# A transformer block with modulation: the first scale load waits on SP until x tile 1 has landed

## The chip, the cores and the metric

The kernel runs on one core of one Trainium2 chip. The metric is the device time of one execution in microseconds (us); three executions of the kernel before took 243.2, 244.03 and 244.05 us, median 244.03. One further execution was recorded by the hardware profiler; all rows of profiles are from such executions.

The engines are named as in the profile: PE (matrix multiply; PEld is its weight load, which overlaps the multiply), DVE (vector), ACT (scalar), POOL (GpSimd) and SP (which here only issues loads and stores). Each has its own list of instructions, which it works through in order, and waits for the others at semaphores.

## The reference

B = 2 sequences of N = 256 tokens, D = 1152, two heads of 576, a hidden width of 4608, all in bf16:

```python
mod = (_silu(c) @ w_mod).reshape(B, 6, 1, D)
shift_a, scale_a, gate_a, shift_m, scale_m, gate_m = [mod[:, i] for i in range(6)]
h = _layernorm(x, axis=-1) * (1 + scale_a) + shift_a
qkv = (h @ wqkv).reshape(B, N, 3, H, Dh)
attn = _softmax(jnp.einsum('bqhd,bkhd->bhqk', q, k) * Dh ** (-0.5), axis=-1)
a = jnp.einsum('bhqk,bkhd->bqhd', attn, v).reshape(B, N, D) @ wo
x = x + gate_a * a
h2 = _layernorm(x, axis=-1) * (1 + scale_m) + shift_m
m = _gelu(h2 @ w_fc1) @ w_fc2
return x + gate_m * m
```

## The kernel before

The 512 tokens are four x tiles of 128 tokens (two for each sequence), each 128 partitions x 1152 columns, 288 KB. The width 1152 is nine chunks of 128. Weights come from device memory into five rotating buffers ("wide"), each holding one 1152 x 1152 matrix.

All instructions of an engine keep the order in which the Python code makes them; a loop at the end of the kernel ties each to the one before it on its engine. So the order of SP's loads is the order of the calls. At the start SP issues:

- the four x tiles, in the order 0, 1, 3, 2 (L85, L86), into `x_sb`;
- then, alternating, the modulation weights that make the attention scale, `w_scale_a`, in five groups of columns (`SGROUPS`: chunks 0-1, 2-3, 4-5, 6-7 and 8; L107), and the rows of the key weights `w_k` that belong to the same chunks (L104, first for the columns of six key panels, the remaining three panels last);
- then the shift and query weights (L129, L134), and through `load_rows` (L120) gate, value and output weights, and later those of the second half of the block.

ACT issues the small load of `c` (L84) and nothing else in this stage. POOL loads nothing in this stage.

The front of the kernel turns x into its normalized, scaled and transposed form and starts the key product at once. `act_stats` (L206) computes the sums of tiles 0 and 2 on ACT, two passes over a tile each; `stats_piece` (L193, L195) those of tiles 1 and 3 on DVE, in three pieces and a closing instruction. From these come the reciprocal deviations: `act_mean_eps` (L213 on DVE, L342 and L218 on POOL), `act_root` (L335) and `root_exp` (L338) on ACT, `pool_rsqrt` (L329) on POOL for tile 3. `norm1` (L233, DVE) writes the normalized tile, PE transposes it by chunks (L264), and `modulate` (L270 on DVE, L272 on ACT) multiplies by the scale into `hT0`.

The scale itself is a product on PE: `scale_group` (L247) multiplies a group of `w_scale_a` columns with silu(c), nine matmuls of two columns for each chunk. So the first group of scale columns is wanted just before the first `modulate`, and `k_step` (L280) then multiplies a chunk of `hT0` with the rows of `w_k` for six key panels. The order in which PE alternates between these is written out by hand (L345 to L404). Before there is work PE runs multiplications of zeros (L173).

After that: the remaining key panels (L309), shift (L416), query (L521), scores, softmax, values (L599), attention output (L640, L693), the second layernorm, and the two large products of the MLP (L746 and L802).

Of the kernel before, what the change touches and what calls it, by code (L numbers as in the profile page):

```python
# [19 lines left out]
def kernel(  # L20
# [11 lines left out]
    nc = tc.nc  # L32
    B, N, D = x.shape
# [3 lines left out]
    P = 128  # L37
    T = B * N
    NT = T // P
    TPB = N // P  # L40
# [9 lines left out]
    WAIT_FOR = mybir.DependencyInfo(mybir.DependencyClass.Sync, mybir.DependencyReason.DATA)  # L50
# [16 lines left out]
    x_v = x.rearrange("b (p l) d -> p b l d", l=TPB)  # L67
    out_v = out.rearrange("b (p l) d -> p b l d", l=TPB)
    c_v = c.rearrange("b (k p) -> (b k) p", p=P)
    wqkv_v = wqkv.rearrange("(k p) n -> p k n", p=P)  # L70
# [7 lines left out]
    def wide_tile(name):  # L78
        return wide.tile([P, KD, D], BF16, name=name, tag="wide")


    x_sb = act.tile([P, NT, D], BF16, name="x_sb", tag="x_sb")
    c_sb = act.tile([B * KD, P], BF16, name="c_sb")
    nc.scalar.dma_start(c_sb[:], c_v)  # L84
    for t in (0, 1, 3, 2):  # L85
        nc.sync.dma_start(x_sb[:, t, :], x_v[:, t // TPB, t % TPB, :])  # L86

    zeros = const.tile([P, T], BF16, name="zeros")
    nc.vector.memset(zeros[:], 0.0)
# [9 lines left out]
    KM1 = 6  # L99
    w_scale_a = wide_tile("w_scale_a")  # L100
    w_k = wide_tile("w_k")

    def load_k(k0, k1, c0, c1):
        nc.sync.dma_start(w_k[:, k0:k1, c0:c1], wqkv_v[:, k0:k1, D + c0:D + c1])  # L104

    for k0, k1 in SGROUPS:
        nc.sync.dma_start(  # L107
            w_scale_a[:, :, k0 * P:k1 * P],
            wmod_v[:, :, S_SCALE_A * D + k0 * P:S_SCALE_A * D + k1 * P],
        )  # L110
        for a, z in [(0, 1), (1, 2)] if k0 == 0 else [(k0, k1)]:
            load_k(a, z, 0, KM1 * P)
    load_k(0, KD, KM1 * P, D)

    first_load = {}

# [279 lines left out]
    for k in range(3, KD):  # L396
        split = 2 if k == 5 else 0
        k_step(k, 0, T, 0, split)
        if k in (3, 5, 7):
            k1 = min(k + 3, KD)  # L400
# [456 lines left out]
```

## Time and profile before

| What | Value |
|---|---|
| Runs, median (lowest to highest) | 244.03 us (243.2 to 244.05) |
| The profiled execution's own time | 243.19 us |
| Its span, first to last instruction | 241.4 us |
| PE busy | 236.4 us (98%) |
| DVE, ACT, POOL busy | 91.4, 59.9, 28.3 us |
| Loads on SP's queue | 50.14 MB, 62.5% of 16 DMA engines' span |
| Granted PE clock | 1.0 |

The span leaves out 1.8 us of the execution that lie before and after it. In the rows of the profile, a group names its line in the code, engine, operation, and the tile it writes and those it reads ("pm<-sT,w_scale_a"), with a count. "SPq" is the issue of a load by SP: its length is the time SP spends on issuing, not that of the transfer. The profile tells separately how long after the start of an issue the data had landed. "Idle before" is the time for which an engine had nothing to do, with what ended it. The chain of waits is followed back from the last instruction; "issue" in it is time in which the engine waited for nothing that the profile shows. Times in rows count from the start of the span, and the first number of a row is the start, the second the length, both in us.

### The profile page before, as it was taken

Reading aid. Unit: us, or ns where it says so; the run is one execution under the profiler, and the core shown is the slowest. Engines: PE = TensorE matmul, PEld = TensorE weight load, DVE = VectorE, ACT = ScalarE, POOL = GpSimd, SP = SyncE. Lnnn points to the kernel's source line nnn. Section 1 sums busy time; section 2 is a strip of 40 time slices with the busy share of each in tenths; the row PEclk is TensorE's granted clock in tenths of the full one; section 3 lists DMA queues with packets and bytes.
Section 4 is the critical chain, followed back from the end, with each engine's and each line's share of the span. In section 5 each row is a group of like instructions: output and inputs, shape, how many; then the busy total and the mean of one; then the engine's idle time right before and its main releaser. Section 6 shows DMA issues by size and latency. Waiting matters only on the chain.

```text
span 241.4 us, 3978 instructions
## 1 busy us (share of the span) xinstructions
PE 236.4 (98%) x1688; PEld 145.1 (60%) x1698; DVE 91.4 (38%) x193; ACT 59.9 (25%) x121; POOL 28.3 (12%) x47
## 2 busy tenths in 40 slices
PE   8999999999999999999999999999999999999994
PEld 5775444466667665888844444444665566666574
DVE  4842442319325678930003999950010000000001
ACT  6723322307215032770423333222000000000000
POOL 2300000001300324100000000001121111111111
PEclk9999999999999999999999999999999999999999
DMA  6999999997499993739999999999300000000000
GB/s 196 325 317 311 377 366 391 391 391 244 122 331 394 389 274 76 195 65 378 391 391 391 337 326 270 287 327 270 98 16 16 20 16 16 19 18 20 26 21 16
DMA packets 48781, 53.29 MB, mean 221 GB/s; under 512 B 9587, under 2 KB 36475, under 8 KB 48763
## 3 DMA queue, kind: packets, MB, share of 16 engines
q1 hardware_dynamic: 41312, 50.14, 62.5%
q10 hardware_dynamic: 6939, 1.71, 4.6%
q0 software_dynamic: 512, 1.19, 1.8%
q8 instruction: 13, 0.21, 0.4%
q14 instruction: 5, 0.04, 0.1%
HBM read 50.14 MB, written 1.19 MB: 213 GB/s over the span
## 4 chain that ended last, share of the span: by engine, by line
PE 94%; issue 2%; ACT 2%; POOL 1%; DVE 0%; POOLq 0%; DVEq 0%; ACTq 0%
PE pacc L802 29%; PE pacc L746 29%; PE pacc L693 7%; PE pacc L599 7%; PE pq L521 7%; PE pk L280 5%; PE pk L309 2%; PE pa L640 2%; PE ps_s L556 2%; PE pn L416 2%; ACT sink L206 1%; PE pt L264 1%; PE pm L247 1%; PE pg L498 0%; ACT rstd L335 0%
## 5 line engine op out<-in xcount | busy, mean ns | idle before, releaser
L746 PE MATMUL pacc<-hT,w_f 128*128 128x256 bf16 (+1 forms) x427 | 70.3, 325 | 0.3
L802 PE MATMUL pacc<-w_f,gT 128*128 128x384 bf16 (+2 forms) x468 | 70.5, 314 | 0.0
L802 PEld LDWEIGHTS <-gT 128*128 128x128 bf16 x468 | 44.4, 98 | 26.3
L746 PEld LDWEIGHTS <-w_f 128*128 128x128 bf16 x432 | 42.2, 98 | 27.6
L808 DVE TENSOR_TENSOR tmp<-pacc,gate 128x384 f32<-128x384 f32 (+2 forms) x13 | 6.8, 526 | 65.6 <-PE pacc L802 57.0
L778 ACT ACTIVATE gT<-pacc 128x512 bf16<-128x512 f32 x24 | 14.3, 597 | 32.7 <-PE pacc L746 32.7
L469 DVE SCALAR_TENSOR_TENSOR part<-w_gate_m,s,part 128x1152 f32<-128x1152 bf16 x16 | 21.4, 1412 | 0.0
L810 POOL TENSOR_TENSOR o_sb<-tmp,x 128x384 bf16<-128x384 f32 (+1 forms) x12 | 11.7, 972 | 53.9 <-DVE tmp L808 53.9
L693 PE MATMUL pacc<-w_o,big 128*128 128x384 bf16 x108 | 17.9, 326 | 0.0
L521 PE MATMUL pq<-hT,w_q 128*128 128x512 bf16 x79 | 17.7, 379 | 0.1
L599 PE MATMUL pacc<-w_v,hT 128*128 128x384 bf16 x108 | 17.7, 326 | 0.0
L599 PEld LDWEIGHTS <-hT 128*128 128x128 bf16 x108 | 10.5, 98 | 7.1 <-issue 0.2
L693 PEld LDWEIGHTS <-big 128*128 128x128 bf16 x108 | 10.4, 98 | 7.2 <-issue 0.4
L521 PEld LDWEIGHTS <-w_q 128*128 128x128 bf16 x81 | 7.8, 98 | 9.4
L280 PE MATMUL pk<-big,w_k 128*128 128x256 bf16 (+1 forms) x70 | 13.1, 324 | 0.1
L699 POOL TENSOR_TENSOR x<-tmp,x_sb 128x384 f32<-128x384 f32 x8 | 7.3, 912 | 27.0 <-DMA w_scale_m<-in_w_mod_dram 15.0
L467 DVE TENSOR_SCALAR part<-w_gate_m,s 128x1152 f32<-128x1152 bf16 x2 | 1.6, 818 | 21.9 <-DMA w_gate_m<-in_w_mod_dram 21.9
L491 POOL DMA_DIRECT2D gates_dram<-nat_v x2 | 1.1, 534 | 67.7 <-DVE nat_v L489 67.7
L280 PEld LDWEIGHTS <-w_k 128*128 128x128 bf16 x72 | 6.7, 97 | 3.7 <-issue 0.3
L767 ACT ACTIVATE gT<-pacc 128x512 bf16<-128x512 f32 x12 | 6.5, 598 | 9.1 <-PE pacc L746 9.1
L173 PE MATMUL pwarm<-zeros 128*128 128x256 f32 x18 | 7.4, 587 | 1.2 <-DVE eps_t L93 1.2
L512 POOL DMA_DIRECT2D gates_dram<-nat x4 | 2.4, 604 | 49.6 <-DVE nat L509 48.5
(102 smaller groups left out, 165.0 us busy)
## 6 DMA issues: line engine op xcount, KB each, us to landing
w_f<-in_w_fc_dram SPq DMA_DIRECT2D x12, 864.0 KB, 14.1
w_f<-in_w_fc_dram SPq DMA_DIRECT2D x3, 1728.0 KB, 7.9
w_f<-in_w_fc_dram SPq DMA_DIRECT2D x2, 2592.0 KB, 17.4
w_gate_a<-in_w_mod_dram SPq DMA_DIRECT2D x3, 864.0 KB, 12.1
w_v<-in_wqkv_dram SPq DMA_DIRECT2D x3, 864.0 KB, 13.8
w_o<-in_wo_dram SPq DMA_DIRECT2D x3, 864.0 KB, 14.0
w_shift_m<-in_w_mod_dram SPq DMA_DIRECT2D x3, 864.0 KB, 8.6
w_scale_m<-in_w_mod_dram SPq DMA_DIRECT2D x3, 864.0 KB, 13.3
```

Of the source, the lines that this page charges most:

```text
L173: nc.tensor.matmul(dst[:, 0:T // 2], zeros32[:, 0:P], zeros32, start=True, stop=True)
L280: nc.tensor.matmul(pk[m][:, c0:c1], w_k[:, k, m * P:(m + 1) * P], hT0[:, k, c0:c1], start=(k == 0 and c0 == 0), stop=(k == KD - 1), skip_g ...
L469: nc.vector.scalar_tensor_tensor(part[:, b, :], wg[:, k, :], s32[:, k, b:b + 1], part[:, b, :], op0=ALU.mult, op1=ALU.add,)
L521: nc.tensor.matmul(pq[m][:], w_q[:, k, m * P:(m + 1) * P], hT[:, k, :], start=(k == 0), stop=(k == KD - 1), skip_group_check=True,)
L599: nc.tensor.matmul(pacc[:], hT[:, k, t * P:(t + 1) * P], w_v[:, k, pnl * PW:(pnl + 1) * PW], start=(k == 0), stop=(k == KD - 1),)
L693: nc.tensor.matmul(pacc[:], aT[:, k, t * P:(t + 1) * P], w_o[:, k, c0:c1], start=(k == 0), stop=(k == KD - 1),)
L699: (nc.gpsimd if pool_add else nc.vector).tensor_tensor(x1[:, t, c0:c1], tmp[:], x_sb[:, t, c0:c1], op=ALU.add)
L746: nc.tensor.matmul(dst, w_f1[m // KD][:, k, ml * P:(ml + 1) * P], hT[:, k, c0:c1], start=start, stop=(k == KD - 1), **kw,)
L778: nc.scalar.activation(gT[:, m, :], pacc[:], ACT.Gelu_apprx_tanh)
L802: nc.tensor.matmul(pacc[:], gT[:, kk, t * P:(t + 1) * P], w_f2[j][:, r, c0 - n * PW:c0 - n * PW + cw], start=(kk == 0), stop=(kk == KF - 1),)
L808: nc.vector.tensor_tensor(tmp[:], pacc[:], gate_m[:, b, c0:c0 + cw], op=ALU.mult)
L810: (nc.vector if last else nc.gpsimd).tensor_tensor(o_sb[:], tmp[:], x1[:, t, c0:c0 + cw], op=ALU.add)
```

## The change

The four x loads keep their order and place, and their handles are kept in a dictionary. The scale and key loads of the loop over `SGROUPS` are kept in a list. One dependency is added: the first of that list, the load of scale columns for chunks 0 and 1, waits for the landing of x tile 1, the second x load that was issued. SP works in order, so every load behind it on SP comes after that wait as well. No data, size or order of a load changes.

```diff
-    for t in (0, 1, 3, 2):
-        nc.sync.dma_start(x_sb[:, t, :], x_v[:, t // TPB, t % TPB, :])
+    x_load = {t: nc.sync.dma_start(x_sb[:, t, :], x_v[:, t // TPB, t % TPB, :]).ins for t in (0, 1, 3, 2)}
...
     def load_k(k0, k1, c0, c1):
-        nc.sync.dma_start(w_k[:, k0:k1, c0:c1], wqkv_v[:, k0:k1, D + c0:D + c1])
-
+        return nc.sync.dma_start(w_k[:, k0:k1, c0:c1], wqkv_v[:, k0:k1, D + c0:D + c1]).ins
+
+    k_loads = []
     for k0, k1 in SGROUPS:
-        nc.sync.dma_start(
+        k_loads.append(nc.sync.dma_start(
             w_scale_a[:, :, k0 * P:k1 * P],
             wmod_v[:, :, S_SCALE_A * D + k0 * P:S_SCALE_A * D + k1 * P],
-        )
+        ).ins)
         for a, z in [(0, 1), (1, 2)] if k0 == 0 else [(k0, k1)]:
-            load_k(a, z, 0, KM1 * P)
+            k_loads.append(load_k(a, z, 0, KM1 * P))
     load_k(0, KD, KM1 * P, D)
+    tc.add_manual_dep(k_loads[0], x_load[1].name, WAIT_FOR, reason="x first")
```

## The prediction

> **What bounds the kernel now.** I read the page's busy times first, then the chain of waits in order of time, the queue of SP, the DMA traffic in half microseconds, and the timeline of the first 32 us. PE is busy 98% of the span. The chain shows where it isn't yet the bound:
>
> ```profile
> 2.46 3.73 issue
> 6.19 0.02 POOLq L218
> ...
> 6.25 0.24 POOL dm L342
> ...
> 7.23 1.25 ACT sink L206 x2
> 8.48 0.02 issue
> 8.50 1.36 ACT sink L206 x2
> ...
> 10.56 0.42 DVE xn L233
> ...
> 11.03 0.29 PE pt L264 x2
> 11.32 0.44 PE pk L280 x4
> ```
>
> Up to 11.03 the end hangs on the layernorm statistics (x tile 0 on ACT, x tile 1 on DVE, then x tile 2 on ACT); from 11.03 on it is PE almost without a break. So a microsecond lost before 11.03, or a PE stall after it, is a microsecond at the end. The change acts here, on SP's own list of issues:
>
> ```profile
> 0.73 1.81 SPq L86 DMA_DIRECT2D x_sb<-in_x_dram  x4
> 2.58 0.43 SPq L107 DMA_DIRECT2D w_scale_a<-in_w_mod_dram  x1
> 3.06 1.67 SPq L104 DMA_DIRECT2D w_k<-in_wqkv_dram  x2
> 4.77 0.60 SPq L107 DMA_DIRECT2D w_scale_a<-in_w_mod_dram  x1
> 5.41 2.25 SPq L104 DMA_DIRECT2D w_k<-in_wqkv_dram  x1
> ```
>
> The four x issues start at 0.73, 1.17, 1.64 and 2.11; asked one by one, they land 2.9, 3.2, 4.6 and 4.9 us later: tile 0 at 3.6, tile 1 at 4.4, tile 3 at 6.2, tile 2 at 7.0. DVE's statistics of tile 1 start at 4.38, which fits. The first scale load is issued at 2.58 and lands 6.4 us later, at 9.0; its first user is PE's load at 9.04:
>
> ```profile
> 4.38 1.48 DVE L193 BATCH_NORM_STATS2 stats<-x_sb 128x6 f32<-128x384 bf16 x3
> ...
> 9.04 0.52 PEld L247 LDWEIGHTS <-w_scale_a 128*128 128x128 bf16 x18
> ...
> 15.19 0.59 PEld L247 LDWEIGHTS <-w_scale_a 128*128 128x128 bf16 x18
> ```
>
> Of the 6.4 us, most is queueing. The DMA traffic (columns: window, its length, busy time of PE, PEld, DVE, ACT, POOL, clock, DMA share, GB/s):
>
> ```profile
> 3.00:3.50 0.50, 0.50 (x3) 0.30 (x3) 0.00 (x0) 0.09 (x1) 0.00 (x0) 1.00 1.03 392
> 3.50:4.00 0.50, 0.50 (x2) 0.41 (x3) 0.34 (x2) 0.46 (x2) 0.00 (x0) 1.00 1.16 281
> 4.00:4.50 0.50, 0.50 (x3) 0.41 (x2) 0.39 (x3) 0.50 (x1) 0.00 (x0) 1.00 1.15 286
> 4.50:5.00 0.50, 0.50 (x3) 0.41 (x2) 0.50 (x2) 0.48 (x2) 0.00 (x0) 1.00 0.82 189
> 5.00:5.50 0.50, 0.50 (x2) 0.41 (x2) 0.50 (x2) 0.48 (x1) 0.00 (x0) 1.00 0.76 256
> ```
>
> With the windows before (81, 218 and 356 GB/s in 1.5 to 3.0) this adds up to 0.5 x 2059 = 1030 KB by 5.5, while the four x tiles are 4 x 288 KB = 1180 KB. In the trace's packet records, where x rows are 2304 bytes, scale rows 512 and key rows 1536, the first 512-byte packet starts at 5.47 and the last x packet ends at 6.60. The weights, issued from 2.58, move no byte before 5.47: the loads of this queue are served in order.
>
> [...] the first x issue starts at 0.73 and the DMA share is 0 until 1.5, with the first x packet at 1.75, so 1.02 us. I use the trace's value.
>
> **The change part by part.** (a) The four x loads are issued as before; gathering their handles in a dictionary and a list adds no instruction. 0.
>
> (b) SP waits after its fourth x issue (2.54) until tile 1 has landed (4.35 to 4.4), so the scale load's issue moves from 2.58 to about 4.40: 1.82 us later. Behind it on SP stand all five scale loads, the seven key loads, the shift and query loads and everything SP loads later; each can go 1.8 us later. Nothing on ACT's or POOL's queue stands behind it. The x tiles 3 and 2 are already issued.
>
> (c) What that does to the data. At 4.40 the queue has moved 0.5 x (81+218+356+392+281) + 0.4 x 286 = 778 KB, so 402 KB of x are left. At the best rate shown (392 GB/s) they last 1.03 us, until 5.43; at the 260 GB/s of the windows behind, until 5.9. The first scale packet comes at 4.40 + 1.02 = 5.42. Before it was 5.47. So the queue does not run dry, or barely: the 1.82 us come out of SP's lead over the data, not out of the data. That lead is the cover. If it were gone, the whole 1.82 us would count.
>
> (d) A cold start is slower than a queue that is fed already. The trace has one with equally many rows (9 rows x 128 partitions): the fc1 load issued at 96.54 onto an idle queue.
>
> ```profile
> 96.54 0.37 SPq L620 DMA_DIRECT2D w_f<-in_w_fc_dram  x1
> ```
>
> It lands 5.0 us later, first traffic in the slot from 97.50. If the time goes by rows, the scale load lands at 4.40 + 5.0 = 9.4, 0.4 late. If it goes by bytes (576 of 864 KB), it lands at 4.40 + 1.05 + 3.95 x 0.67 = 8.1, 0.9 early. By the queue's view in (c) it lands at 9.0. Bounds of its lateness: -0.9 to +0.4; I take +0.1.
>
> (e) What lateness costs. At PE's 9.04 there is no slack on the scale load itself. But what PE and DVE do next ends in waits for ACT: DVE sits idle 0.2 us for ACT's rstd before the tile 2 normalization at 10.56, and PE's loads 0.4 us before 11.03. So 0.2 us of lateness are free there. After that PE never idles; the next tight place is the scale load for columns 4-5, issued at 7.71, landing 7.4 us later (15.1) and used at 15.19: slack 0.1. Columns 6-7 land at 10.96 + 7.2 = 18.2 for 18.98, column 8 at 21.4 for 22.08, the first shift load at 18.39 + 10.2 = 28.6 for 29.31. The first query load lands at 20.14 + 11.4 = 31.5 for 31.79. A lag of 0.4 that lasted to 15.1 would cost 0.3; a lag of 0.1 costs 0 to 0.05.
>
> (f) SP's lead afterwards. From first scale to second scale issue SP needs 4.77 - 2.58 = 2.19 us, for 960 KB (983 thousand bytes); at the 320 GB/s that the queue then moves these take 3.07 us. So SP gains 0.88 us on the data for every such round, and has its old lead back after about two rounds (1.82 / 0.88), near 11 us. Meanwhile the lead doesn't go below the first packet's 1.02 us: the second scale load, issued at 4.77 + 1.82 = 6.6, can move from 7.6; its turn comes after 983 thousand bytes from 5.45, at 8.5. Cost 0.
>
> (g) A possible gain: x flows at 392 GB/s until 3.5, then at 189 to 286, just from one first-packet latency behind the scale issue (2.58 + 1.02 = 3.6). [...] the change takes that off, and tile 1 lands up to 0.2 earlier. DVE's chain leads ACT's by little: ACT's second pass over tile 0 ends at 6.37, and ACT starts its root at 6.51 because POOL's epsilon came at 6.48. So at most 0.14 us. Tiles 3 and 2 would land earlier by 0.5 to 1.5 us for nothing: ACT is busy until 7.22 before tile 2 (7.0), DVE until 6.14 before tile 3 (6.2). Bounds -0.14 to 0; I take 0.
>
> The sum is 0 (a) + 0.1 at most of (b to e) + 0 (f) + 0 (g): +0.1, within -0.14 and +0.4. The profiled execution has span 241.4 and 1.8 around it, 243.19; it becomes 243.3. The runs' median, 244.03, lies 0.84 above that execution; taken over, the forecast is 244.1.
>
> **The rivals.** *The queue runs dry* (slower). If a restarted queue needs longer than the x that is left to drain, the stream slides as a block: the scale load keeps its 6.4 us, lands at 10.8, PE stands at 9.04 and again at 15.19, and the end moves by 1.82 - 0.05 = 1.8 us: 245.8. For it: the cold start at 96.54 reaches only 135 GB/s in its second quarter microsecond. Against it: 402 KB of x at 4.40 and the first weight byte at 5.47. It decides once the first-packet latency passes some 1.5 us (5.9 - 4.4), and costs what lies above; a partial version, with 0.5 to 1 us lost, gives 244.5 to 245.0.
>
> *x arrives earlier* (g): 0.14 less, 243.9. For it: the rate's fall at 3.5. Against: the two issues behind tile 1 can't speed up tile 0, whose ACT passes carry the chain.
>
> *Faster by more than 1.2 us*: this would need a piece of the front to vanish. The chain's x wait before ACT's first pass ends at 3.63 on tile 0, which the change leaves alone; after it, ACT's own four passes of 1.25 us fill the time. Worked out, nothing gives under 243.9 by mechanism.
>
> **How the numbers follow.** A change of 0.5% (1.2 us) is about what a measurement here can tell from none: the runs before span 243.2 to 244.05. Forecast as it stands, 0.62; x earlier, 0.10; the partial slide, 0.10; the full slide, 0.14; faster by over 0.5%, 0.04. The first three are within 0.5%, 0.82. The range reaches from 243.0, the lower run less the 0.14 of (g), to 245.2, the partial slide with its margin; it leaves out the full slide and the large gain, 0.18.
>
> **What would show it.** Right: SP's scale issue at about 4.4, first PE load of the scale weights at 8.9 to 9.3, DMA traffic without an empty window between 5 and 6, PE's second dense stretch still from about 11.0, and the load for columns 4-5 used at 15.1 to 15.4. (g) shows as tile 2 landing near 5.6 and 350 GB/s or more in 3.5 to 5.0. The slide shows as a window near 0 GB/s around 5.5 and PE's loads at 10.8. The forecast is wrong if tile 1 is seen landing later than 4.4, if the restart needs over 1.5 us, or if the lead is not regained before 15 us.

## The result, and the profile after

The changed kernel takes 245.29 us (median of 6 executions, 244.7 to 245.78); the kernel before, in the same comparison, 243.88. The ratio is 1.006, 95% interval 1.004 to 1.0081: 1.4 us slower, where 0.1 was forecast and the range ended at 245.2. The profiled execution took 244.91 us with a span of 243.1, 1.7 more than the span of before.

SP's issues in the profile after (start, length):

```profile
0.73 1.80 SPq L85 DMA_DIRECT2D x_sb<-in_x_dram  x4
4.38 0.38 SPq L107 DMA_DIRECT2D w_scale_a<-in_w_mod_dram  x1
4.81 1.87 SPq L103 DMA_DIRECT2D w_k<-in_wqkv_dram  x2
6.72 0.43 SPq L107 DMA_DIRECT2D w_scale_a<-in_w_mod_dram  x1
7.20 1.81 SPq L103 DMA_DIRECT2D w_k<-in_wqkv_dram  x1
```

The wait does what the diff says: the first scale load leaves at 4.38, 1.80 us later than before, and the scale and key loads behind it 1.3 to 2.1 later. It lands 5.9 us after its issue, at 10.3; before it was 9.0. PE's loads of scale weights, with the idle time ahead of them in brackets:

```profile
10.31 0.52 PEld L248 LDWEIGHTS <-w_scale_a 128*128 128x128 bf16 x18 [1.44 <-DMA w_scale_a<-in_w_mod_dram]
...
13.94 0.52 PEld L248 LDWEIGHTS <-w_scale_a 128*128 128x128 bf16 x18 [0.45 <-DMA w_scale_a<-in_w_mod_dram]
...
16.98 0.52 PEld L248 LDWEIGHTS <-w_scale_a 128*128 128x128 bf16 x18 [0.28 <-DMA w_scale_a<-in_w_mod_dram]
```

Before, these stood at 9.04, 12.30 and 15.19 with no wait on a load. They are now 1.27, 1.64 and 1.79 later. From the third on nothing more is gained or lost: the last large product stands at 169.68 in the chain of waits, in place of 167.96, 1.72 later. So the whole difference of the two profiles arises in the first 17 us. The chain of waits says the same; ACT's statistics have left it, and loads stand there:

```profile
1.16 3.21 DMA x_sb<-in_x_dram
...
4.38 0.38 SPq L107
...
6.72 7.17 DMA w_scale_a<-in_w_mod_dram
...
13.95 0.60 PE pm L248 x18
...
16.98 0.60 PE pm L248 x18
```

The DMA traffic (the last number is GB/s; columns as in the prediction) shows what the landing hides. Before:

```profile
5.50:6.00 0.50, 0.50 (x2) 0.34 (x2) 0.47 (x2) 0.50 (x1) 0.00 (x0) 1.00 0.96 293
6.00:6.50 0.50, 0.50 (x3) 0.39 (x2) 0.42 (x3) 0.36 (x2) 0.25 (x2) 1.00 1.03 321
6.50:7.00 0.50, 0.50 (x3) 0.41 (x2) 0.50 (x2) 0.48 (x2) 0.23 (x1) 1.00 1.08 328
7.00:7.50 0.50, 0.50 (x3) 0.41 (x2) 0.50 (x2) 0.48 (x2) 0.00 (x0) 1.00 1.17 339
```

After:

```profile
5.00:5.50 0.50, 0.50 (x2) 0.41 (x2) 0.50 (x2) 0.47 (x1) 0.00 (x0) 1.00 0.66 254
5.50:6.00 0.50, 0.50 (x2) 0.35 (x2) 0.47 (x2) 0.50 (x1) 0.00 (x0) 1.00 0.66 113
6.00:6.50 0.50, 0.50 (x3) 0.45 (x2) 0.50 (x3) 0.37 (x2) 0.23 (x2) 1.00 0.74 195
6.50:7.00 0.50, 0.50 (x4) 0.44 (x3) 0.50 (x3) 0.47 (x2) 0.25 (x1) 1.00 0.98 270
7.00:7.50 0.50, 0.50 (x4) 0.43 (x3) 0.50 (x2) 0.47 (x3) 0.00 (x0) 1.00 1.08 305
```

No window is empty, and the first 512-byte packet starts at 5.44, as forecast (5.47 before). But behind it the rate takes some 2 us to climb from 113 to 305 GB/s. From 8 to 12 it is 231, 258, 274 and 263 GB/s against 336, 322, 292 and 338.

Summed over 1.5 to 12, x's faster flow gains 125 KB before 5.5. Then 256 KB are lost up to 8.0 and 262 KB more up to 12, some 390 KB net: 1.2 us at 322 GB/s. This is one execution; a second profile of the same kernel, further down, lost less.

A second thing stands in the list of executions. The PE clock that was granted on average over the whole execution was 0.998 or 1.0 in three of the six (244.7 to 244.98 us) and 0.992 in the other three (245.6 to 245.78).

### The profile page after: what moved, and what is told of

It is laid out like the page before. It is cut to its first block, busy times and chain, and to the rows that moved or that the text cites. A ratio compares the mean times of both kernels' runs of the same rounds, so it can differ in the third digit from the quotient of the medians.

```text
span 243.1 us, 3988 instructions
## 1 busy us (share of the span) xinstructions
PE 236.8 (97%) x1698; PEld 144.6 (59%) x1698; DVE 91.3 (38%) x193; ACT 59.9 (25%) x121; POOL 28.4 (12%) x47
## 4 chain that ended last, share of the span: by engine, by line
PE 93%; DMA 4%; SPq 1%; DVE 0%; issue 0%; DVEq 0%
PE pacc L747 29%; PE pacc L803 29%; PE pacc L694 7%; PE pacc L600 7%; PE pq L522 7%; PE pk L281 4%; DMA w_scale_a<-in_w_mod_dram 3%; PE pk L310 2%; PE pa L641 2%; PE ps_s L557 2%; PE pn L417 2%; DMA x_sb<-in_x_dram 1%; PE pm L248 1%; SPq L103 1%; PE pt L265 1%; PE pg L499 0%
## 5 line engine op out<-in xcount | busy, mean ns | idle before, releaser
L174 PE MATMUL pwarm<-zeros 128*128 128x256 f32 x18 | 6.8, 546 | 1.2 <-DVE eps_t L92 1.2
```

Of the source, the lines that this page charges most:

```text
L174: nc.tensor.matmul(dst[:, 0:T // 2], zeros32[:, 0:P], zeros32, start=True, stop=True)
```

## The experiments

Each edit is one to the changed kernel, except for one run of the kernel before; times are ratios to the kernel before, measured on the same chip. "+" times are the ratio applied to that kernel's median. All of them compute the full result.

### How long may SP be held?

The wait of the changed kernel, with another tile:

```diff
-    tc.add_manual_dep(k_loads[0], x_load[1].name, WAIT_FOR, reason="x first")
+    tc.add_manual_dep(k_loads[0], x_load[0].name, WAIT_FOR, reason="x first")
```

> The first scale load waits on x tile 0 (lands at 3.6) in place of tile 1, so SP is held 1.05 us instead of 1.82. Theory L (what SP is held is lost one for one[...]): first scale load 1.0 later than in the kernel before, PE's columns 4-5 about 1.0 later than 15.2, time +0.9 to +1.0 us. Theory R (a restart of the queue costs a fixed amount, whatever the hold): as in the changed kernel, +1.4 to +1.7. Theory Q of the prediction (only an empty queue costs): 0, at 3.6 some 640 KB of x are left.

Measured: 0.9996 (0.9982 to 1.001), no difference. SP resumes at 3.76, 1.2 us late; the scale load lands at 9.2, and PE's third load of scale weights is 0.15 from where it was (15.19):

```profile
9.27 0.52 PEld L248 LDWEIGHTS <-w_scale_a 128*128 128x128 bf16 x18 [0.32 <-DMA w_scale_a<-in_w_mod_dram]
12.39 0.61 PEld L248 LDWEIGHTS <-w_scale_a 128*128 128x128 bf16 x18
15.34 0.52 PEld L248 LDWEIGHTS <-w_scale_a 128*128 128x128 bf16 x18
```

Theory L and theory R both fall here: 1.2 us of holding cost nothing that shows (0.2 us at most), and 0.6 more cost the 1.4.

With `x_load[2]`, the last tile:

> The first scale load waits on x tile 2, the last one (lands at about 6.5 when no weights are behind it), so SP is held about 3.9 us and the queue runs empty for certain. Theory L: +3.7 to +4.0 us. Theory R: the fixed restart cost of 1.4 to 1.7 plus the empty time, about 2.1 us more than in the changed kernel, so +3.6 to +3.8 too: this run alone doesn't part the two. Theory Q: only the empty time, first scale packet at 7.6 in place of 5.5, so +2.0 to +2.2.

Measured: 1.0101 (1.0079 to 1.0123), +2.5 us. SP resumes at 6.82 onto an empty queue; the scale load lands 4.3 us later, at 11.1, sooner after its issue than in the changed kernel (5.9). L and R, at +3.6 and more, fall again; Q's +2.0 to +2.2 lies within the interval.

With `x_load[3]`:

> The first scale load waits on x tile 3 (lands at 5.6 to 5.9 when no weights are behind it), 1.2 to 1.5 us later than for tile 1. Theory H ([...] 5.9 us from issue to landing, against 4.3 us on the empty queue of the run that waits for tile 2): the scale load lands about 4.4 us after its issue, near 10.1 to 10.3, as in the changed kernel, and the time is +1.3 to +1.8. Theory R (a restart costs its fixed amount on top of the hold): scale load near 11.6, +2.6 to +3.0.

Measured: 1.0086 (1.0067 to 1.0105), +2.1 us. The landing is theory H's, 4.6 us after the issue at 5.63, at 10.2. The time in the median lies between H and R, but two of the four executions are at a PE clock of 0.992 and 0.993; the other two took 245.10, 1.5 us more than the kernel before, as H has it. Why the load takes longer behind the draining x tail (5.9 us in the changed kernel) than here, no run shows. The restart of an empty queue can be seen here by itself (columns as above):

```profile
6.00:6.50 0.50, 0.50 (x3) 0.39 (x2) 0.50 (x3) 0.41 (x2) 0.22 (x1) 1.00 0.00 0
6.50:7.00 0.50, 0.50 (x3) 0.46 (x2) 0.50 (x2) 0.45 (x2) 0.27 (x2) 1.00 0.65 41
7.00:7.50 0.50, 0.50 (x4) 0.43 (x3) 0.50 (x2) 0.47 (x3) 0.00 (x0) 1.00 0.56 84
7.50:8.00 0.50, 0.50 (x4) 0.33 (x2) 0.47 (x3) 0.50 (x1) 0.08 (x1) 1.00 0.80 225
8.00:8.50 0.50, 0.28 (x3) 0.03 (x2) 0.42 (x2) 0.50 (x2) 0.42 (x2) 1.00 0.98 295
```

First packet at 6.68, 1.05 us after the issue; then 1.5 us up to full rate. At 330 GB/s the load's 590 thousand bytes take 1.8 us; its packets took from 6.68 to 9.67, 3.0. So in this run the restart cost 1.05 us to the first packet and about 1.2 more behind it.

### Is it the hold, or what is queued meanwhile?

The wait on tile 1, on the second load in the list (`k_loads[1]`, the first key load):

> The wait on x tile 1 sits on the second load (the first key load); the first scale load is issued freely at 2.58. SP is held from 3.06 to 4.4, 1.3 us. Theory L (SP's lag is what counts): +1.2 us, scale columns 2-3, 4-5 and so on each 1.3 later. Theory C (what counts is how much is queued in the rings while SP is held; here 590 thousand bytes of scale weights stand behind x, until about 7.3): 0, within 0.3 us, first scale load at 9.0 as before.

Measured: 1.0 (0.9988 to 1.0012). The wait for tile 2 on the second scale load (`k_loads[3]`, `x_load[2]`):

> The wait sits on the second scale load and is for x tile 2 (about 7.0); first scale load and the first two key loads go freely. SP is held from 4.77 to 7.0, 2.2 us, more than in the changed kernel. Theory L: +2.0 to +2.2 us. Theory C: the queue then holds x and 983 thousand bytes of weights, until about 8.5, and the next packet can come at 8.0: 0 to +0.3 us.

Measured: 0.9991 (0.9979 to 1.0004). SP's issues there:

```profile
2.57 0.43 SPq L107 DMA_DIRECT2D w_scale_a<-in_w_mod_dram  x1
3.05 1.62 SPq L103 DMA_DIRECT2D w_k<-in_wqkv_dram  x2
6.56 0.38 SPq L107 DMA_DIRECT2D w_scale_a<-in_w_mod_dram  x1
6.98 0.98 SPq L103 DMA_DIRECT2D w_k<-in_wqkv_dram  x1
8.01 0.67 SPq L107 DMA_DIRECT2D w_scale_a<-in_w_mod_dram  x1
```

SP stands still from 4.67 to 6.56, no shorter than in the changed kernel (1.89 and 1.85 us), and is within 0.3 us of its place two loads later (8.01, before 7.71). This settles it against theory L: a hold of this length can be free. The difference from the changed kernel is that here 983 thousand bytes of weights had been issued behind x when the hold began.

### Do the short rows make it?

First the key loads ahead of the scale load, without and with the wait:

```diff
     for k0, k1 in SGROUPS:
+        if k0 == 0:
+            k_loads.append(load_k(0, 1, 0, KM1 * P))
+            k_loads.append(load_k(1, 2, 0, KM1 * P))
         k_loads.append(nc.sync.dma_start(
...
-        for a, z in [(0, 1), (1, 2)] if k0 == 0 else [(k0, k1)]:
-            k_loads.append(load_k(a, z, 0, KM1 * P))
+        if k0 > 0:
+            k_loads.append(load_k(k0, k1, 0, KM1 * P))
```

> No wait; the first two key loads (128 rows of 1536 bytes each) stand ahead of the first scale load (1152 rows of 512 bytes). The scale load then lands about 1.1 us later than in the kernel before (393 thousand bytes at 350 GB/s), near 10.1, so PE starts 1.1 us later: +0.9 to +1.1 us. It serves as the base of the next run.

> As the run before, with the wait on x tile 1 on the first key load: SP is held 1.82 us as in the changed kernel, but the first thing it issues is two loads with few long rows. Theory D (the loss comes from starting with many short rows[...]): 0 to +0.4 us over the run without the wait. Theory R (any restart at this point costs about as much): +1.2 to +1.7 over it.

Measured: 1.0022 (1.0009 to 1.0035) without the wait, +0.5 us and less than expected; 1.0141 (1.0126 to 1.0156) with it. The 2.9 us between the medians are more than either theory has: all four executions with the wait are at a PE clock of 0.991 to 0.993. The same loads at full clock (the run with `fill(11)` below) are 1.3 us over the run without the wait. That is R's amount, and theory D falls. The key loads themselves land only 0.3 and 0.2 later than without the wait, but the scale load behind them 1.4 later (11.7, not 10.3).

Then wider groups, so that a scale row has 1024 bytes, with six multiplications of zeros on PE (`fill(6)`) ahead of the first scale product:

```diff
-    SGROUPS = [(0, 2), (2, 4), (4, 6), (6, 8), (8, 9)]
+    SGROUPS = [(0, 4), (4, 8), (8, 9)]
...
-        for a, z in [(0, 1), (1, 2)] if k0 == 0 else [(k0, k1)]:
+        for a, z in [(0, 1), (1, 2), (2, 4)] if k0 == 0 else [(k0, k1)]:
```

> No wait; scale columns come in groups of four, four and one chunks, so that the rows of the first scale load are 1024 bytes in place of 512 (1152 rows as before, 1180 thousand bytes), with six multiplications of zeros ahead of the first scale product. The first scale load lands about 1.8 us later than before, near 10.8: +1.2 to +1.8 us. It is the base of the next run.

> The run before with the wait on x tile 1 on the first scale load. Theory D2 (the loss is that short rows come at some 400 to 560 rows a microsecond [...]: 512 bytes each are then 220 to 290 GB/s, 1024 bytes each would be over 400): 0 to +0.5 us over the run without the wait. Theory R (a restart costs the same whatever the rows): +0.9 to +1.5 us over it.

Measured: 1.0063 (1.004 to 1.0087) and 1.017 (1.0144 to 1.0197), 2.9 us between the medians. Four of the five executions with the wait are at a clock of 0.990 to 0.993, none of those without; the fifth took 246.87, 1.7 us over the median without. That one too is far over D2's 0 to 0.5: longer rows don't help. The first scale load lands 1.9 us later with the wait (12.8, 10.9).

The trace has sixteen increments of a semaphore for each load, the steps by which its landing is counted. Which part of the transfer an increment stands for, it doesn't show. In the run with wide groups and the wait four come at 12.4 to 12.8, all others by 11.3. In the changed kernel's first scale load two come at 10.0 and 10.3, all others by 8.9. Landing waits for the last: PE's load of scale weights starts at 10.31, the last increment is at 10.27. In the kernel before, the whole load had landed at 8.98; so fourteen of the sixteen were on time in the changed kernel, and the lateness of this landing is that of two. Its second profile, next, says the same: fourteen by 8.98, the others at 9.4 and 10.0.

### What does PE's stall cost, and why do executions differ by 0.9 us?

The changed kernel once more:

> The changed kernel once more, beside the others on one chip. If its profile is typical: scale load issued at 4.4 and landing near 10.3, [...] PE waits of 1.4, 0.4 and 0.3 us on scale loads, +1.2 to +1.7 us. If the late landing was one execution's accident, the scale load lands near 9.0 to 9.4 here and the cost sits in the later loads.

Measured: 1.0052 (1.0034 to 1.007), +1.3 us. The scale load lands at 10.0; PE waits 1.03 us for it and 0.34 for the third:

```profile
10.02 0.52 PEld L248 LDWEIGHTS <-w_scale_a 128*128 128x128 bf16 x18 [1.03 <-DMA w_scale_a<-in_w_mod_dram]
...
16.17 0.52 PEld L248 LDWEIGHTS <-w_scale_a 128*128 128x128 bf16 x18 [0.34 <-DMA w_scale_a<-in_w_mod_dram]
```

The traffic dips as in the first profile (230 KB lost from 5.5 to 8.0), but from 8 to 12 only 26 KB are lost. Net of the gain before 5.5 that is 135 KB, 0.4 us. PE's last product is 0.9 us later than before, and the profiled execution is the fastest of the eight. So the slow stretch from 8 to 12 belongs to the first execution; the dip, the two late increments and the wait for the third load are in both. One of eight executions had a clock of 0.993, and it was the slowest (245.71).

PE filled with multiplications of zeros while it waits:

```diff
+    fill(5)
     pm0, pm1 = [scale_group(k, k + 1, acc_tile) for k in range(2)]
```

> The changed kernel with five multiplications of zeros (about 1.1 us) ahead of the first scale product, so that PE is not idle while it waits for the late scale load. Theory T (two costs add: late scale loads, and in some executions a lowered PE clock after an idle PE): no execution under a clock of 0.995, median +0.9 to +1.2 us against the kernel before, highest run within 1 us of the lowest. Without T (the clock is not of the idle PE's making): executions of 0.992 to 0.993 and of 1.0 to 1.5 us more remain as frequent as in the changed kernel (4 of 14).

> The kernel before with the same five multiplications, loads untouched: only PE's start on the first scale product moves, from 9.05 to about 10.1. It prices the first stall by itself. By the prediction's slack of 0.2 us: +0.8 us. If scale loads later on have slack to give back, less; if PE's place at 15.19 is what counts (slack 0.1, load not late here) the stall still reaches it in full, so +0.8 either way. Same as before would mean that the first late scale load is not what costs the changed kernel its time.

Measured for the changed kernel: 1.0039 (1.0027 to 1.0051), +0.95 us, 244.11 to 245.03, all twelve executions at a clock of 0.998 or more. In the profiled one, the fastest, the first scale load landed at 9.1, before the zeros were done, and PE still waited 0.3 us for the third (16.02) and 0.5 for the fourth. For the kernel before: 1.001 (0.9999 to 1.0021), +0.2 us, not the 0.8 expected, though PE starts on the first scale product 0.92 later:

```profile
9.96 0.52 PEld L247 LDWEIGHTS <-w_scale_a 128*128 128x128 bf16 x18
12.92 0.61 PEld L247 LDWEIGHTS <-w_scale_a 128*128 128x128 bf16 x18
15.78 0.61 PEld L247 LDWEIGHTS <-w_scale_a 128*128 128x128 bf16 x18
```

In this profile the 0.92 have become 0.59 at 15.78 (before: 15.19), and the fastest executions differ by as much (243.71 and 243.14). The medians differ by less, so part of that stall is probably there in many executions of the kernel before; in this one the load itself landed only at 9.5. A stall of 0.92 us at the first scale product by itself thus costs 0.2 us in the median. In all three profiles of the changed kernel, with and without the zeros, PE waits again for the third scale load, at 16.0 to 17.0. Most of the 0.95 us is therefore likely to come from the later loads; how late the first one was in executions without a profile is not known.

In the run with the key loads first and the wait, PE's idle time was longest, and its profile shows the clock (third number from the end of a row):

```profile
11.00:12.00 1.00, 0.28 (x11) 0.29 (x12) 0.00 (x0) 0.00 (x0) 0.00 (x0) 1.00 1.12 284
12.00:13.00 1.00, 1.00 (x18) 0.68 (x15) 0.83 (x5) 0.00 (x0) 0.00 (x0) 0.67 0.96 301
13.00:14.00 1.00, 1.00 (x7) 0.69 (x6) 0.33 (x2) 0.00 (x0) 0.00 (x0) 0.50 1.05 295
14.00:15.00 1.00, 1.00 (x8) 0.76 (x7) 0.19 (x1) 0.00 (x0) 0.00 (x0) 0.50 1.14 307
15.00:16.00 1.00, 1.00 (x7) 0.79 (x6) 0.88 (x3) 0.47 (x1) 0.00 (x0) 0.62 1.09 333
```

PE had been idle for 2.84 us up to 11.71. Then it gets half its clock, and does 7 to 8 matmuls a microsecond. A window with mean 0.67 has two thirds of a microsecond at 0.5, one with 0.62 three quarters: in all 3.4 us at half clock. The same with `fill(11)` at that place:

> The run with the key loads first and the wait on the first of them, with eleven multiplications of zeros (2.4 us) where PE stood idle for 2.8 us. Loads are as there. Theory T (idle PE lowers its clock to 0.5 for about 3 us afterwards): no execution under 0.995, and 0.8 to 1.3 us less than without the multiplications, 245.6 to 246.1. Without T: 246.7 to 247.0 as there.

Measured: 1.0075 (1.0063 to 1.0088), 245.26 to 245.47 in all five executions, clock 0.999 or more, against 246.7 to 247.0 at 0.991 to 0.993 without: 1.6 us less with the first loads as late as before (scale load at 11.5). The same windows:

```profile
12.00:13.00 1.00, 0.91 (x14) 0.78 (x13) 0.96 (x5) 0.00 (x0) 0.00 (x0) 1.00 1.11 317
13.00:14.00 1.00, 0.99 (x11) 0.70 (x9) 0.60 (x3) 0.09 (x1) 0.00 (x0) 1.00 1.05 304
```

And the run that waits on tile 3, with `fill(6)`:

> The run that waits on x tile 3, with six multiplications of zeros (1.3 us) ahead of the first scale product. Theory T: no execution under 0.995 (two of four were), median at the level of its undisturbed executions, 245.1 or little less. Theory G for its loads: 2.1 us missing, +1.5 to +2.1 against the kernel before.

Measured: 1.0073 (1.0059 to 1.0087), +1.8 us, no clock under 0.998 (two of four without the fill). What theory T says of the clock came true in all three; the saving of 1.6 us is more than its 0.8 to 1.3. The half clock came here after 2.84 us of idle time. It came after 1.40 (1.49 for the weight load), with 1.22 two microseconds earlier, in the profile of the run with the wait on tile 3 in the next section:

```profile
10.44 0.52 PEld L251 LDWEIGHTS <-w_scale_a 128*128 128x128 bf16 x18 [1.49 <-DMA w_scale_a<-in_w_mod_dram]
...
12.00:13.00 1.00, 1.00 (x7) 0.78 (x6) 0.06 (x1) 0.00 (x0) 0.00 (x0) 0.50 1.05 370
```

The length of one idle time doesn't decide it, though. The run that waits for the last tile stood idle for 2.2 us in its profile, and none of its four executions had a low clock. The wide groups with the wait had six zeros, but PE stood idle for another 2.6 us behind them in the profile, which shows no low clock; the four other executions had one. The kernel before had a low clock, 0.993, in 3 of the 102 executions measured beside these runs.

### How much must be queued?

From the runs so far theory G was formed: 1.05 us to the first packet and 1.1 behind it must be covered by what is still queued when SP resumes; what is missing is lost. Two more runs, with the key loads first and going freely and the first scale load waiting (`k_loads[2]`), for tile 1 and for tile 3:

> Order as in the run with the key loads first; the two key loads go freely, and the first scale load behind them waits on x tile 1. SP is held from 3.5 to 4.3, 0.8 us. Theory G (when SP resumes, the queue must still hold about 2.1 us of data, 1.05 to the first packet and 1.1 for the slow start behind it; what is missing is lost): at 4.3 about 400 thousand bytes of x and 393 thousand of keys are queued, 2.2 us at 360 GB/s, so nothing is missing: the same as with the key loads first and no wait, ratio 1.002 to the kernel before, within 0.15%.

> As the run before, waiting on x tile 3 (about 5.3 to 6.4). SP is held 1.8 to 2.9 us. Theory G: the queue then holds the keys and a tail of x, 1.2 to 1.7 us, so 0.4 to 0.9 us are missing: +0.4 to +0.9 us over the run with the key loads first and no wait, +0.9 to +1.4 over the kernel before. If any wait that leaves the queue non-empty were free: 0. If the hold were lost one for one: +1.8 to +2.9.

Measured: 1.0055 (1.0032 to 1.0079) and 1.0083 (1.006 to 1.0107), both slower than expected, but mixed with the clock: four of nine and four of five executions are at 0.991 to 0.993. The executions at 0.998 or more are 243.96 to 244.79 (median 244.2, ratio 1.0027) and a single 244.28; the run with the key loads first and no wait had 1.0022 in all. That is G's forecast for the first and less than its 0.4 to 0.9 for the second, but five and one picked executions don't carry a verdict.

The profiles, both of low-clock executions, are against G as a rule for landings. With the wait for tile 1 some 840 thousand bytes were queued when SP resumed at 4.41 (issued, less the packets done), and the scale load landed 0.8 later than without the wait (11.1, 10.3), two increments last again. With the wait for tile 3 some 300 thousand were queued at 6.14, and it landed only 0.1 later. By the bytes that the queue had moved in all, the two streams were later by 0.3 and 0.7 us, nearer to G's 0 and 0.4 to 0.9.

Set against the other waits, G asks for nothing with the waits on the second load and on the second scale load (0 measured), 0.4 us with tile 0 (0 measured, 0.2 at most), 1.05 with tile 1 (0.95 with PE filled) and with the key loads first (1.3 with PE filled), 2.1 with tile 3 (1.8 with PE filled) and 2.5 with the last tile, whose queue had been empty for 0.4 us (2.5). Of these only the 1.8 was forecast by G before it was measured; the 1.05 and 1.1 come from these runs themselves. G doesn't explain the 1.9 us by which the wide scale load came late. It is a rule of thumb for this queue, not shown as the cause.

## Why the prediction was wrong

**Parts (a) and (b)** held: SP resumed at 4.38, tile 1 landed where forecast, and SP's scale and key loads went 1.3 to 2.1 us later.

**Part (c) is the step that failed**, and with it the lateness in (d). The arithmetic held: first scale packet forecast at 5.42, measured 5.44. The inference "out of SP's lead over the data, not out of the data" did not: a first packet on time was taken for a stream on time. Behind it came 113 to 305 GB/s in place of 293 to 339, and the data were 1.2 us late by 12 us in one profile, 0.4 in the other. The tiles' last 402 KB covered the 1.05 us to the first packet, but not the slow stretch behind it. Whether the kernel before has such a slow start too, hidden under the x data since its scale load was issued at 2.58, no run shows.

**Part (d)** had a slow start in view, in the load at 96.54 (65, 135, 255 and 255 GB/s in the quarters of a microsecond from 97.50), and bounded the lateness at +0.4; +0.1 was chosen because (c) seemed to say so. Measured: +1.3, and +1.0 in the second profile. The upper bound was passed because two increments fell behind the fourteen that were on time (by 8.90 and 8.98, before 8.98). A cold restart on an empty queue does not show this: the sixteen increments of the load at 96.54 lie within 0.8 us.

**Part (e)** was near: 0.2 us of slack forecast, and in the filled kernel before 0.92 us of delay at PE's first scale product cost 0.59 in the profile and 0.2 in the median.

**Part (f) failed on its result, not on its mechanism.** Forecast: lead regained near 11 us and the later loads at cost 0. With enough queued SP does come back near its place (8.01 against 7.71 in the run that holds the second scale load). In the changed kernel the data themselves were behind, and SP's issue at 15.78 was still 1.82 late. The load for columns 4-5 landed at 16.9 in place of 15.1 (16.1 in the second profile), and PE's third load of scale weights moved by 1.79 (0.98): it is from there that the end of both profiles is late.

**Part (g)**: x did flow faster, 336, 304 and 378 GB/s in 3.5 to 5.0 against 281, 286 and 189, and tiles 3 and 2 landed 0.3 and 0.4 earlier (0.04 and 0.07 in the second profile). It brought nothing, as argued.

**What was missing** is PE's clock: the prediction puts it at nothing. It is low (0.992 or 0.993) in 4 of 14 executions (245.6 to 245.78, the ten others 244.1 to 245.22 with median 244.8), in none of the 12 with the idle time filled. That is some 0.9 us each, 0.25 on average, and in the comparison behind the result, with three of six, more. The late loads by themselves cost 0.95 us (the run with PE filled). The two together come to about the 1.3 to 1.4 us measured. The range's end, 245.2, was passed by 0.1 in the first comparison and not reached in the second (244.78), and the forecast of no change failed in both.

**The rivals.** "The queue runs dry" named the right place and too late a point: it put the decision at a first-packet latency of 1.5 us, which was 1.06. Its price, 1.8 us, is near the 1.72 that PE lost in the first profile, and its partial version (244.5 to 245.0) holds the median of the executions at full PE clock, 244.8. Its picture of a stream that slides as a block, with one lateness for all, is not what the increments show.

What stays open is why single increments fall behind. The last increment of the first scale load comes 1.2 to 2.1 us after the middle ones in six of the seven profiles in which SP resumes with or just ahead of it at 4.3 to 4.4 (0.6 in the seventh, the filled changed kernel). It comes 0.2 to 0.9 us after them in the five in which SP resumes at 3.8 or after 5.6. Where SP doesn't wait ahead of this load, it is 0.7 to 1.3 us in six profiles. So single late increments are not the wait's doing alone. Neither row length nor order of loads prevents the lag; no run here shows its cause.

## What to carry to other kernels

A wait on the issuing engine can cost nothing or more than a microsecond, and its length alone doesn't tell which. Here holds of 1.2 to 1.9 us were free with 600 thousand to a million bytes queued when SP resumed, and holds of 1.8 us cost about 1 us with 400 to 440 thousand; one profile with 840 thousand queued was late all the same. Look at the rate behind the first packet, and at a load's last increment, not at the first packet alone. And when a change leaves PE idle for a microsecond or more, ask what its clock does afterwards (0.5 for 3.4 us in three profiles here); work of zeros that fills the whole gap is cheap (0.2 us in the median of the kernel before).

## What the runs showed of the hardware

- A load issued onto this queue after a pause needed 1.05 us from issue to first packet (1.05 to 1.06 in the runs that wait for tiles 1, 2 and 3). On an all but empty queue it then took about 1.5 us from 41 GB/s up to 295 (the run that waits for tile 3).
- The same load of 590 thousand bytes landed 4.3 to 4.6 us after its issue on an empty or all but empty queue (three profiles), 4.8 to 5.9 behind a draining one (four), and 6.4 to 6.9 when issued well ahead (four).
- A load's landing waits for the last of its sixteen increments, and two alone made it a microsecond late in both profiles of the changed kernel: fourteen were in by 8.90 and 8.98, the last at 10.27 and 9.97.
- PE's clock went to 0.5 for 3.4 us after idle times of 2.84, 2.20 and 1.40 us, in one profile each, and stayed at 1.0 after 2.16 and 2.60 us in two others. The clock was low in all four executions of the first of these kernels. It stayed at 0.998 or more in all 22 executions of the three waiting kernels whose gap was filled by multiplications of zeros.
